# Full-row weights for one-row matmuls, crossbar transposes at two block boundaries, and another emission order, in a fused state-space and gated-MLP kernel

## Chip, cores and metric

One core of one Trainium2 chip. The metric is device time in microseconds (us) from start to end of one execution.

PE is TensorE's matmul side, PEld its weight load, DVE VectorE, ACT ScalarE, POOL GpSimd, SP the engine that issues DMAs here (SPq is its queue). L480 is line 480 of the kernel concerned. The kernels with padding have one line more above the matmuls, so L480 of the kernel before is L481 there.

## The reference

A pre-normalized state-space convolution with a residual, then a pre-normalized gated MLP with a residual, for 2048 positions of 640 channels:

```python
# u: (1, 2048, 640); A, B, C: (640, 128) complex
P = jnp.exp(logdA[:, :, None] * l[None, None, :])
K = jnp.einsum("dn,dnl,dn->dl", Cc, P, dB).real        # the taps
y = irfft2(rfft2(pad(u)) * rfft2(pad(K)))[..., :L] + u * Dskip
# ... cut ...
h  = x + ssm(layernorm(x))
h2 = h + (sigmoid(layernorm(h) @ w_gate) * (layernorm(h) @ w_up)) @ w_down   # F = 1728
```

## The kernel before

The kernel has two stages. Stage one builds tables and taps on DVE, ACT and PE, transforms the input (`forward`) and the taps (`spec`), and inverts block 0 of the result. Stage two runs the MLP on four blocks of 512 positions, in whose gaps PE inverts the next block from spectral products (`VR`) that DVE makes.

One-row matmuls: `one`, `last` and `sel` pick rows; `one` adds the skip term to tap 0, `last` adds edge taps, `sel` adds the edge term of block 0's last position.

```python
    sel[32, 0, 31] = 1.0
    # ... cut ...
    for c in range(4):
        last[c, 0, c, 0:4] = 1.0
        last[c, 1, c, 4:10] = 1.0
        last[c, 2, c, 10:14] = 1.0
    one[64, 0] = 1.0

        def diagonal(g1, kts):                       # 8 calls
            ps = ps2.tile([P, 2, 512], F32, name="ps_kv", tag="p2")
            # ... cut ...
            for c4 in range(4):
                for m in range(4):                   # L479: 128 rows, 32 columns
                    MM(pv[32 * m:32 * m + 32, :, :, c4], lhsT=pick[:, c4, :], rhs=kj[:, :, :, 4 * m + c4], start=not c4, stop=(m > 0 and c4 == 3), tile_position=(0, 32 * m))
            MM(pv[0:32, 0], lhsT=one[64:65, :], rhs=edge[64:65, dc]..., start=False, stop=True, tile_position=(64, 0))     # L480
            # ... cut: L482 ...
            nc.scalar.copy(kv[:, :, 4 * g1:4 * g1 + 4 * GC], ...)
            for q in range(2):                       # L485
                MM(ps[0:NL, 1, 0:4 * GC], lhsT=last[0:1, q, 0, :], rhs=kv[0:1, 3 + q, ...], start=False, stop=(q == 1))

    def inv0(c, ...):                                # 4 calls
        # ... cut ...
            if a:                                    # L550
                MM(ps[96:128, a, W:2 * W], lhsT=sel[32:33, 0, :], rhs=edge[32:33, o:o + W], start=False, stop=False, tile_position=(32, 96))
```

The order of stage one: every piece of work is a named unit with needs; of the units whose needs are met, the one with the lowest key in a table `AT` is emitted next. `s0` is the spectrum of the first 160 channels' taps for one lag, `l0` the same for the other lags, `p0` their product with the input's spectrum; `f1` and `f2` are the forward transforms of blocks 1 and 2.

```python
            unit(f"s{c}", f"k{c}d S01 f0 n0", L(corner, c), L(spec, c, 0, 0), L(spec, c, 0, 1))
            unit(f"p{c}", f"s{c}" + ..., L(prod, c, (0, 1)))
            unit(f"l{c}", f"s{c}", ...)              # spec of lags 1 to 3
    unit("ea1", "A1", L(exps_a, 1))                  # a burst of ACT exponentials
    units["ivh"] = (["f1", "f2"], (mk_iv,))
```

The boundary from one MLP block to the next. `DT` says for each block whether the crossbar transposes the normalized rows, `PW` which PSUM buffers are used:

```python
    def turn(b):
        lnT = lnTs[b] = xp.tile([P, 5, 4, 128], BF16, name="lnT", tag="G")
        if AT["DT"][b]:
            for i in range(4):
                nc.sync.dma_start(lnT[:, :, i, :], ln2[:, i, :], transpose=True)
            return
        if b and AT["PW"]:
            pts = [pso[0].tile([P, 4, 4, 128], BF16, name="ml_pt", tag="ml_po") for _ in range(2)]
            # ... 20 transposes on PE, three ACT copies ...
            return
        # ... otherwise five pieces of 4 transposes and a copy, in the gate's buffers ...

        for lp in (0, 2):                            # the down projection's halves
            if lp and AT["PW"]:                      # second half in the gate's and up's buffers
                po = [[p.tile(...) for _ in range(2)] for p, t in ((psg_p, "ml_pg"), (psu_p, "ml_pu"))]
            else:                                    # in the down projection's own two buffers
                po = [[t[:, c] for c in range(2)] for t in (pso_p.tile(...) for _ in range(2))]
            if not lp and b < NB - 1:
                prep(b + 1)                          # layer norm of the next block
            chunks(0, True, False)
            if lp and b < NB - 1:
                turn(b + 1)
            # ... 64-row tail, chunks(1, False, True) ...
            # ... for k, c:
                        tb = Wd[:, 15, 320 * c:320 * c + 320]
                        nc.scalar.copy(tb, po[k][c][:, 0:320])
```

## Time and profile before

| | before |
|---|---|
| time, median (range of four runs) | 361.31 us (360.59 to 361.48) |
| span of the profiled execution | 358.8 us |
| first large inverse of block 0 starts (L556) | 116.34 us |
| last inverse of block 0 has ended (first statistics of its result, L718) | 145.35 us |
| gate projection starts, blocks 1, 2, 3 (L898) | 206.26, 260.69, 310.71 us |
| last spectral products for block 3, start of the pair (L695) | 283.79 us |

These milestones are read from the timeline. They are a row of posts along the chain that ends last: a difference that appears between two posts was made there. Each is read from one execution. The busy shares and the chain are in the prediction. Columns of a timeline are start, duration, engine, line, operation, output and inputs, count, and in brackets the idle time ahead and what ended it.

### The profile page before, as it was taken

The numbers are of one execution on the slowest core, as the hardware profiler recorded it, in microseconds if no ns is written. First come the engines' busy times: TensorE is split into PE (matmuls) and PEld (weight loads), VectorE is DVE, ScalarE is ACT, GpSimd is POOL, SyncE is SP. The second block draws the span as 40 slices with busy tenths as digits, with TensorE's granted clock in tenths as the row PEclk, the third lists the DMA queues.
The fourth block names the chain that finished last, engine by engine and source line by source line (L and its number), as shares of the span: only waits on it lengthen the run. The fifth ranks groups of instructions, "written<-read, shape, count | busy, mean of one in ns | idle before, by whom it ended". The sixth has DMA issues, their size and how long they took to land.

```text
span 358.8 us, 6679 instructions
## 1 busy us (share of the span) xinstructions
PE 324.9 (91%) x2604; PEld 205.7 (57%) x2604; DVE 285.4 (80%) x597; ACT 245.0 (68%) x449; POOL 11.6 (3%) x19
## 2 busy tenths in 40 slices
PE   1598979899999999899999899998699999999995
PEld 1385646777586769744456544455444556644463
DVE  4899999999999979789998999998999931221221
ACT  6999997999899645662767755656655578655500
POOL 1011102000000000100001000001000001000000
PEclk9999999999999999999999999999899999999999
DMA  6990000257007159799400250000030000100011
GB/s 178 337 379 3 16 2 2 83 158 266 13 3 221 75 183 357 177 291 299 184 4 0 74 186 36 2 0 2 1 146 3 0 0 2 55 20 1 0 37 38
DMA packets 29703, 34.37 MB, mean 96 GB/s; under 512 B 16988, under 2 KB 25053, under 8 KB 29416
## 3 DMA queue, kind: packets, MB, share of 16 engines
q1 hardware_dynamic: 29672, 33.95, 29.1%
q8 instruction: 20, 0.33, 0.4%
q14 instruction: 11, 0.09, 0.1%
HBM read 24.72 MB, written 9.21 MB: 95 GB/s over the span
## 4 chain that ended last, share of the span: by engine, by line
PE 41%; DVE 32%; ACT 13%; DMA 7%; issue 3%; SPq 2%; POOL 1%; POOLq 0%; DVEq 0%; ACTq 0%
PE ml_pg L898 8%; PE ml_pu L898 8%; PE ml_po L931 6%; DVE u L684 4%; DVE u L685 4%; PE ps_z L449 3%; PE ps_y L556 3%; PE ps_xk L510 3%; DVE u L687 2%; DVE u L688 2%; PE ps_kv L479 2%; PE pk L468 2%; DVE ln_st L399 2%; ACT zs L450 2%; DMA raw<-in_A_C_re_dram 2%
## 5 line engine op out<-in xcount | busy, mean ns | idle before, releaser
L898 PE MATMUL ml_pg<-lnT,Wg 128*128 128x512 bf16 x260 | 64.8, 379 | 0.7 <-ACT ml_sg L906 0.7
L898 PE MATMUL ml_pu<-lnT,Wu 128*128 128x512 bf16 x260 | 64.9, 379 | 0.5 <-ACT Wd L952 0.4
L931 PE MATMUL ml_po<-Wd,ml_hm 128*128 128x320 bf16 x416 | 59.1, 301 | 0.0
L931 PEld LDWEIGHTS <-ml_hm 128*128 128x128 bf16 x416 | 40.1, 98 | 18.7 <-issue 2.4
L906 ACT ACTIVATE ml_sg<-ml_pg 128x512 bf16<-128x512 f32 x52 | 31.2, 599 | 26.0 <-PE ml_pg L898 14.6
L909 DVE TENSOR_TENSOR ml_hm<-ml_ub,ml_sg 128x512 bf16<-128x512 bf16 x52 | 21.8, 419 | 28.4 <-ACT ml_ub L908 28.4
L908 ACT CAST ml_ub<-ml_pu 128x512 bf16<-128x512 f32 x52 | 30.4, 585 | 20.4 <-PE ml_pu L898 20.2
L898 PEld LDWEIGHTS <-Wu 128*128 128x128 bf16 x260 | 25.4, 98 | 31.5 <-issue 1.0
L898 PEld LDWEIGHTS <-Wg 128*128 128x128 bf16 x260 | 25.4, 98 | 29.2 <-issue 0.9
L449 PE MATMUL ps_z<-u,c_G 128*128 128x320 bf16 x192 | 28.8, 298 | 2.2 <-ACT a_cs L273 0.7
L510 PE MATMUL ps_xk<-kv,c_KM 128*128 128x160 bf16 x320 | 26.6, 232 | 2.4 <-ACT zs L450 1.0
L684 DVE TENSOR_TENSOR u<-Z,S 128x1280 bf16<-128x1280 bf16 x34 | 27.7, 817 | 0.1
L685 DVE TENSOR_TENSOR u<-Z,S 128x1280 bf16<-128x1280 bf16 x34 | 27.7, 816 | 0.0
L246 PE MATMUL ps_t<-fr,c_dg 128*128 128x160 f16 (+1 forms) x180 | 20.0, 240 | 6.1 <-DMA c_dg<-s4c_dg 4.3
L510 PEld LDWEIGHTS <-c_KM 128*128 128x128 bf16 x320 | 23.1, 98 | 4.1 <-issue 3.2
L449 PEld LDWEIGHTS <-c_G 128*128 128x128 bf16 x192 | 18.4, 97 | 10.9 <-issue 3.9
L246 PEld LDWEIGHTS <-c_dg 128*128 128x128 f16 x180 | 14.8, 100 | 13.0 <-issue 4.9
L688 DVE TENSOR_TENSOR u<-u,u 128x1280 bf16<-128x1280 bf16 x23 | 18.8, 817 | 0.0
L687 DVE TENSOR_TENSOR u<-u,u 128x1280 bf16<-128x1280 bf16 x23 | 18.8, 816 | 0.0
L468 PE MATMUL pk<-tabB,tabA 128*128 128x84 bf16 x320 | 16.6, 200 | 2.3 <-ACT kts L469 2.0
L468 PEld LDWEIGHTS <-tabA 128*128 128x128 bf16 x320 | 14.4, 97 | 5.2 <-issue 4.3
L469 ACT CAST kts<-pk 128x420 bf16<-128x420 f32 x32 | 15.6, 543 | 2.5 <-PE pk L468 2.4
(157 smaller groups left out, 549.6 us busy)
## 6 DMA issues: line engine op xcount, KB each, us to landing
dz<-zs SPq DMA_DIRECT2D x12, 320.0 KB, 2.2
c_KM<-s4c_KM SPq DMA_DIRECT2D x1, 2560.0 KB, 12.8
dxk<-xk SPq DMA_DIRECT2D x16, 160.0 KB, 2.4
h<-in_A_u_dram SPq DMA_DIRECT2D x4, 640.0 KB, 3.9
eo<-dz SPq DMA_DIRECT2D x4, 640.0 KB, 4.6
S<-dxk SPq DMA_DIRECT2D x4, 640.0 KB, 7.4
Wg<-in_B_w_gate_dram SPq DMA_DIRECT2D x4, 520.0 KB, 7.9
Wu<-in_B_w_up_dram SPq DMA_DIRECT2D x4, 520.0 KB, 7.7
```

Source lines behind the costliest of these rows:

```text
L246: MM(ps[:, a, q * w:q * w + w], lhsT=dg[:, dk, :], rhs=fr[:, src, i, o + oo:o + oo + w], start=False, stop=(q == m - 1 and i == 1))
L449: MM(ps[:, ri, 0:UH], lhsT=G[:, ft, 0 if b in EO else hf, ri, r, :], rhs=us[b][:, r, o:o + UH], start=(r == rr[0]), stop=(r == rr[-1]))
L468: MM(pk[:, i, :], lhsT=A[:, ri, g].rearrange("p e c -> p (e c)"), rhs=B[:, ri, :, 4 * g:4 * g + 4], start=(ri == 0), stop=(ri == 1))
L510: mm = MM(ps[:, hf, ri * W:ri * W + W], lhsT=KM[:, ft, hf, ri, KI[d] + q, :], rhs=kv[:, j, :], start=(q == 0), stop=(q == len(KD[d]) - 1)).ins
L684: V(t1, z, k[:, :, :, hs_], ALU.mult)
L685: V(t2, z, k[:, :, ::-1, hs_], ALU.mult)
L687: V(s1, s1, t1, ALU.add)
L688: V(s2, s2, t2, ALU.add)
L898: nc.tensor.matmul(ps[:], lhsT=W[:, dc, f0:f0 + 128], rhs=lnT[:, dc].rearrange("p a b -> p (a b)"), start=(dc == 0), stop=(dc == 4))
L906: nc.scalar.activation(sg[:], pg[:], AF.Sigmoid)
L908: nc.scalar.copy(ub[:], pu[:])
L931: nc.tensor.matmul(po[k][c][:, 0:320], lhsT=hm[:, ft, 128 * lr:128 * lr + 128], rhs=Wd[:, ft, 320 * c:320 * c + 320], start=(start and ft ...
```

## The change

The intent: give the one-row matmuls all rows, with zero weights for those that do not matter, so that their weight loads need not idle ahead of them (0.37 us for L480 in the kernel before); take the transposes of blocks 2 and 3 off PE and ACT; and re-order stage one to suit. The diff, with `AT` cut (49 of its 59 keys change):

```diff
-AT = {... "bb2": 68.1, "ea1": 70.7, "ta2": 71.2, "s0": 66.5, "l0": -14.7, "p0": -14.4, "PW": 1,
-      "DT": (0, 0, 0, 0), "NA": (1, 2, 0, 0), "SA": (2, 0, 0, 3), "F": (-18.0, 64.3, 14.3, 46.5), ...}
+AT = {... "bb2": 68.7, "ea1": 70.7, "ta2": 72.8, "s0": 71.3, "l0": -17.5, "p0": 54.3, "PW": 0,
+      "DT": (0, 0, 1, 1), "NA": (1, 0, 1, 2), "SA": (1, 0, 0, 3), "F": (-59.9, 64.3, 14.3, 80.5), ...}
     for c in range(4):
-        last[c, 0, c, 0:4] = 1.0
-        last[c, 1, c, 4:10] = 1.0
         last[c, 2, c, 10:14] = 1.0
+    last[0, 0, 0, 0:4] = 1.0
+    last[0, 1, 0, 4:10] = 1.0
     edge = cp.tile([96, D], BF16, name="edge")
+    nc.gpsimd.memset(edge[:], 0.0)
-            MM(pv[0:32, 0], lhsT=one[64:65, :], rhs=edge[64:65, dc]..., tile_position=(64, 0))
+            MM(pv[0:32, 0], lhsT=one[0:96, :], rhs=edge[:, dc]..., tile_position=(0, 0))
-                MM(ps[0:NL, 1, 0:4 * GC], lhsT=last[0:1, q, 0, :], rhs=kv[0:1, 3 + q, ...], ...)
+                MM(ps[0:NL, 1, 0:4 * GC], lhsT=last[:, q, 0, :], rhs=kv[:, 3 + q, ...], ...)
-                MM(ps[96:128, a, W:2 * W], lhsT=sel[32:33, 0, :], rhs=edge[32:33, o:o + W], ..., tile_position=(32, 96))
+                MM(ps[96:128, a, W:2 * W], lhsT=sel[0:96, 0, :], rhs=edge[:, o:o + W], ..., tile_position=(0, 96))
-                        tb = Wd[:, 15, 320 * c:320 * c + 320]
+                        tb = Wd[:, 14 + k, 320 * c:320 * c + 320]
```

## The prediction

2.9 - 0.5 + 2.4 = 4.8 us, less 1.2 for the cap, plus 1.0 come to 4.6, so 361.4 - 4.6 = 356.8. "Drain" is what the trace shows at L480, an idle weight load of 0.37 us and 0.2 us of chain; that rows make it, and that all rows remove it, was inferred from the waits told beside it. The 0.15 for a pair of L485 was an estimate. The 0.07 of streaming is the pace of other 160-column matmuls of this trace (52 of L510 in 3.89 us). "For columns it shows" speaks of the trace, "This trace has none" of crossbar transposes.

> **What bounds the kernel now.** The kernel was timed at 361.38 us (median of three runs); its profiled execution spans 358.8 us. I read first the page's busy shares and its row of slices, then the table of 10-us stretches, then the chain of waits, and last the timeline of the places that the diff touches. Line numbers are those of the kernel before.
>
> ```profile
> PE 324.9 (91%) x2604; PEld 205.7 (57%) x2604; DVE 285.4 (80%) x597; ACT 245.0 (68%) x449; POOL 11.6 (3%) x19
> PE   1598979899999999899999899998699999999995
> DVE  4899999999999979789998999998999931221221
> ACT  6999997999899645662767755656655578655500
> ```
>
> There are two stages. In stage one (to about 149 us: tables, kernel taps, forward transforms, the inverse of block 0) PE, DVE and ACT are all nearly full. From the 10-us stretches, PE idles about 11 us between 20 and 150 us and DVE about 6.6 us. In stage two (four blocks of layer norm, gate and up projection, down projection) PE is full except at block boundaries, and DVE is full until about 285 us with the spectral products that later blocks need.
>
> The chain runs through DVE up to 51 us, through a mix of ACT and PE up to about 115 us, and from there to 145 us nearly only through PE. That is where the one-row matmuls stand (L480 and L485; L550 is the third kind):
>
> ```profile
> 118.73 0.86 PE ps_kv L479 x14
> 119.59 0.14 PE ps_kv L480
> 119.73 0.17 PE ps_kv L482 x2
> 119.98 0.76 PE ps_kv L479 x12
> 120.74 0.13 PE ps_kv L480
> 120.88 0.25 PE ps_kv L482 x4
> ```
>
> The timeline of the same place has the weight load of the one-row matmul idle for 0.37 us, not for data but for "issue", and the wait table repeats it for all three lines:
>
> ```profile
> 119.52 0.09 PEld L480 LDWEIGHTS <-c_one 1*32 1x32 bf16 x1 [0.37 <-issue]
> ```
>
> ```profile
> PEld L480 <- issue: 2.4, 7, 0.4
> ...
> PEld L485 <- issue: 1.4, 4, 0.4
> ...
> PEld L550 <- issue: 0.8, 3, 0.3
> ```
>
> In stage two the largest wait of PE is for the layer norm's transposes: "PE ml_pt L863 <- ACT Wd L952", 4.6 us in three waits: 1.8 us ahead of block 1, 2.7 ahead of block 2, 0.2 ahead of block 3. The boundary from block 1 to block 2:
>
> ```profile
> 253.50 0.72 ACT L952 CAST Wd<-ml_po 128x320 bf16<-128x320 f32 x2
> 254.28 1.87 PE L863 MATMUL ml_pt<-c_ident,ln 128*128 128x128 bf16 x16 [2.66 <-ACT Wd L952]
> 256.07 2.42 ACT L865 COPY lnT<-ml_pt 128x1024 bf16<-128x1024 bf16 x3 [1.85 <-PE ml_pt L863]
> 256.72 4.13 PE L931 MATMUL ml_po<-Wd,ml_hm 128*128 128x320 bf16 x26
> 260.69 1.24 PE L898 MATMUL ml_pg<-lnT,Wg 128*128 128x512 bf16 x5
> ```
>
> PE needs a buffer that ACT empties only after four normalizations (they end at 253.6), then transposes, then finishes the down projection, then starts block 2.
>
> [...] 0.26 to 0.37 us of idle load ahead of one-row and 64-row matmuls (L480, L485, L550, L942). For columns it shows next to nothing: L479 (128 rows, 32 columns) follows full-array matmuls without a recorded wait. So padding to all rows should remove the drain although the outputs stay 32 columns wide. [...] This trace has none; its nearest relative is an SBUF-side copy of the same 160 KB in rows of 320 bytes, which landed in 2.4 us:
>
> ```profile
> dxk<-xk SPq DMA_DIRECT2D x16, 160.0 KB, 2.4
> ```
>
> **The change part by part.** (1) Padding. 8 matmuls L480, 8 pairs L485 and 4 matmuls L550 get all rows (96 or 128), with zero weights. [...] The groups of four L479 start every 0.19 us (118.83, 119.02, 119.21), so L480 could have started at 119.40 and started at 119.53: 0.13 of drain. Its successor came 0.13 later where 0.05 is usual: 0.08. That is 0.2 us for one L480. I estimate 0.15 for a pair of L485 (0.16 in the chain [...]) and 0.2 for L550 (0.17 in the chain where 0.07 is streaming, plus what precedes it). Sum: 8 x 0.2 + 8 x 0.15 + 4 x 0.2 = 3.6 us of PE time. On the PE-only part of the chain after 115 us are 4 of each: 4 x 0.55 = 2.2 us. Of the other 1.4 I count half, as ACT often ends the wait there: 0.7. Together 2.9 us off stage one, if DVE follows. The cleared edge tile costs one GpSimd memset near the start, beside idle time.
>
> (2) Emission order. I compared what each engine does before fixed points, with this trace's durations. DVE's work before the first tap product (which opens the PE part) is 52.1 before and 51.8 after (nominal sums; operations overlap by about a tenth). One more statistics row and one normalization fewer on DVE add 0.8 nominal, about 0.7 us by the end of stage one. ACT loses about 1 us there, PE nothing. The number of ACT table loads stays four. So the order as such brings no work off any engine; I count it as +0.5 us, with an uncertainty of 2 to 3 us, because it may close or open some of DVE's 6 us of waits.
>
> (3) Transposes. Blocks 2 and 3 lose 20 transposes each on PE and three ACT copies (2.42 us), and get four crossbar DMAs each. The second half of each down projection now accumulates in the same two buffers as the first, in every block, not in the gate and up buffers. At the boundary to block 2: PE finishes its first half at 250.9 minus 3.6 = 247.3; the first buffer is emptied at 248.56, so PE waits 1.3 us, works 3.6 us to 252.2, and waits for the second buffer to 254.2 (the copies at 253.50). Then tail and last half, 0.4 + 3.6 us: free at 258.2 where before it was 260.7. Gain 2.4 us, if the transposes have landed by then. The last normalized row is there at 253.6, so they have 4.6 us; from the 2.4 us of the copy I expect 3 us for the last. At the boundary to block 3: transposes cost 1.4 us (305.25 to 306.80, less the down projection's own start), a new wait for the second buffer 0.3: gain 1.0 us, with 4.7 us of room. At the boundary to block 1 the transposes stay on PE, but in five pieces through two buffers, interleaved with five ACT copies; it loses about 0.5 us and saves the 0.4 us wait of the first up projection for its buffer: nothing. Block 3's end has no ACT copies and does not change. Sum: 3.4 us.
>
> **The cap.** PE can move forward only as far as DVE's products do.
>
> ```profile
> 283.79 0.88 DVE L695 TENSOR_TENSOR VR<-y 128x640 bf16<-128x640 bf16 x2
> ```
>
> They end at 284.67, and PE reads them in the third inverse group of block 2 at 286.60: 1.9 us of slack. Up to there the parts sum to 2.9 - 0.5 + 2.4 = 4.8 us. DVE must then come 2.9 us earlier, out of some 9 us of waits, with 0.7 us more work. I count 1.2 us of the 4.8 as lost to it: 3.6. With the 1.0 at the boundary to block 3: 4.6 us, so 361.4 - 4.6 = 356.8.
>
> **Rivals.** (a) Slow crossbar. [...] At three times the plain copy, 7 us for the last, each boundary gives back 2.4 us: about 361. [...] a tuned schedule that keeps such a loss is unlikely. (b) DVE is the bound. Its row is full from 20 to 285 us; then padding only turns PE work into PE waits for products, and the gain is the 1.9 us of slack and the 1.0 after it, less 0.7: about 359. (c) The drain is worth more than I read, or the new order packs DVE's waits well: all of the 3.6 us, and 4 of DVE's 9 us: about 351. (d) The column mode drains too once the row mode does not: part 1 is nothing, about 358.5.
>
> **Range and chances.** Rivals (b) and (d) lie within 2 us of the prediction; (c) is the lower end, a mildly slow crossbar the upper. Predicted 356.8 us, 8 in 10 between 351 and 363. Faster by over 2% means under 354.15, which needs 7.2 us: 0.21. Slower by over 2% means over 368.6, which needs the slow crossbar: 0.06. Within 2%: 0.73.
>
> **What would show it.** Right: no "issue" wait ahead of the loads of the padded matmuls, and about 0.2 us less at each on PE; PE's largest wait in stage two now for the down projection's buffer (1 to 3 us at the boundary to block 2); transposes landing within 4.6 us of the last normalization; a new or longer PE wait for VR in block 2. Wrong: gate matmuls of blocks 2 and 3 waiting for a DMA; the padded matmuls still idle for "issue"; stage one's end (the last block-0 inverse, 145.3 us now) earlier by over 5 us or later than now, which would make the emission order the main term.

## More of the kernel before

Every execution told here was at a mean granted TensorE clock of 0.99 to 1.00.

The kernel before:

```profile
62.05 1.79 PE L449 MATMUL ps_z<-u,c_G 128*128 128x320 bf16 x12 [0.17 <-ACT tabMB L273]
63.68 1.82 PE L510 MATMUL ps_xk<-kv,c_KM 128*128 128x160 bf16 x24
66.55 3.89 PE L510 MATMUL ps_xk<-kv,c_KM 128*128 128x160 bf16 x52 [1.04 <-ACT zs L450]
70.59 0.44 PE L510 MATMUL ps_xk<-kv,c_KM 128*128 128x160 bf16 x4 [0.16 <-ACT xk L514]
71.19 4.01 PE L449 MATMUL ps_z<-u,c_G 128*128 128x320 bf16 x28 [0.16 <-ACT xk L514]
```

Two kinds of work alternate: forward transforms (L449) and spectra of the taps (L510, units `s0` and `l0`, 80 matmuls here). The bracketed waits sum to 1.5 us.

## The result, and the profile after

The changed kernel ran in 358.73 us (median; 357.72, 358.83, 358.74, 358.71) against 361.31 before. The ratio is 0.9926, 95% interval 0.9904 to 0.9948. Ratios here are the mean time of one kernel's fast runs over that of the other's of the same rounds, so not quite the ratio of the medians. Correct, and inside 2%. The span of the profiled execution went from 358.8 to 355.9 us.

| milestone (start, us) | before | after | difference |
|---|---|---|---|
| first large inverse of block 0 | 116.34 | 118.31 | +1.97 |
| last inverse of block 0 has ended | 145.35 | 145.51 | +0.16 |
| gate of block 1 | 206.26 | 206.46 | +0.20 |
| gate of block 2 | 260.69 | 258.15 | -2.54 |
| gate of block 3 | 310.71 | 307.73 | -2.98 |

So stage one brought nothing, although PE should have had 2.9 us less to do there; the whole gain was made at the boundaries to blocks 2 and 3. The busy shares of the kernel after:

```profile
PE 322.0 (90%) x2564; PEld 203.5 (57%) x2564; DVE 286.2 (80%) x600; ACT 239.9 (67%) x442; POOL 11.0 (3%) x20
```

**The boundary to block 2.** The timeline of the kernel after:

```profile
251.16 5.29 SPq L858 DMA_TRANSPOSE lnT<-ln  x4
...
253.47 0.72 ACT L953 CAST Wd<-ml_po 128x320 bf16<-128x320 f32 x2
254.25 0.43 PE L943 MATMUL ml_po<-Wd,ml_hm 64*128 64x320 bf16 x3 [1.11 <-ACT Wd L953]
...
254.61 3.71 PE L932 MATMUL ml_po<-Wd,ml_hm 128*128 128x320 bf16 x26
258.15 1.03 PE L899 MATMUL ml_pg<-lnT,Wg 128*128 128x512 bf16 x4
```

PE's transposes are gone; what holds PE now is the copy that empties the down projection's buffer, for 1.11 us, as predicted. The SP queue spends 5.29 us on issuing four transposes of 128x640, 1.22 to 1.33 us each; the single plain DMAs on it from 200 to 310 us take 0.24 to 0.36 us each. The table of DMAs of the kernel after shows that each transpose landed about as fast as the plain copy of 160 KB (2.4 to 2.5 us):

```profile
lnT<-ln SPq DMA_TRANSPOSE x8, 2.6
```

Part of the gain here is the clock, which the prediction did not count. In a table of stretches the columns are the stretch, its length, the busy time of PE, PEld, DVE, ACT and POOL with instruction counts, then the granted clock, the DMA share and GB/s. The kernel before, just after PE's wait of 2.66 us:

```profile
254.00:256.00 2.00, 1.72 (x16) 1.60 (x15) 2.00 (x6) 0.23 (x1) 0.00 (x0) 0.55 0.00 0
```

The kernel after, in an earlier stretch behind PE waits of 0.31 and 1.22 us, and in the same one:

```profile
244.00:246.00 2.00, 2.00 (x9) 1.18 (x9) 2.00 (x6) 1.46 (x3) 0.00 (x0) 0.50 0.00 0
...
254.00:256.00 2.00, 1.75 (x14) 1.11 (x14) 2.00 (x5) 0.95 (x3) 0.00 (x0) 1.00 0.73 147
```

At the lower clock the kernel before took 1.87 us for 16 transposes (1.05 ahead of block 3), 0.71 for the tail (0.45 there) and 4.13 for the 26 matmuls that take 3.71 after: about 1.5 us. In the kernel after the low stretch costs nothing: from the gate of block 1 to that of block 2 it takes 51.69 us, and so does the kernel e, told below, whose clock is 1.00 from 242 to 248 us.

**The padding.** The chain of the kernel after, at the place whose chain before is in the prediction:

```profile
120.69 0.87 PE ps_kv L480 x12
121.56 0.02 PE ps_kv L481
121.58 0.08 PE ps_kv L483 x2
...
121.75 0.76 PE ps_kv L480 x13
122.50 0.04 PE ps_kv L481
122.54 0.16 PE ps_kv L483 x4
```

The one-row matmul's own step in the chain fell from 0.13 to 0.14 us to 0.02 to 0.04 us. From 118.73 to the end of the last step the chain took 2.40 us before; here, from 120.69 to 122.70, it took 2.01: 0.2 us less for each L480, the predicted size. The weight-load waits tell more. In the kernel after (columns: total us, times, longest) there is no such wait left for L481, where there were 2.4 us in seven, but the two other padded kinds are still there:

```profile
PEld L486 <- issue: 0.8, 2, 0.4
PEld L551 <- issue: 0.8, 3, 0.3
```

In the chain, a pair of L486 takes 0.17 us (122.85), as a pair of one-row L485 did (0.16), and L551 takes 0.17 as L550 did. L486 has fewer such waits than L485 (1.4 us in four), but in the kernel d, told below, it has 1.1 us in three. Only one of the three kinds got its gain.

**Stage one's middle.** PE of the kernel after in the 62 to 76 us shown above for the kernel before:

```profile
61.77 2.20 PE L450 MATMUL ps_z<-u,c_G 128*128 128x320 bf16 x15
65.59 4.01 PE L450 MATMUL ps_z<-u,c_G 128*128 128x320 bf16 x28 [1.62 <-ACT zs L451]
69.76 2.33 PE L450 MATMUL ps_z<-u,c_G 128*128 128x320 bf16 x16 [0.15 <-ACT zs L451]
72.82 2.20 PE L450 MATMUL ps_z<-u,c_G 128*128 128x320 bf16 x15 [0.73 <-ACT zs L451]
75.84 0.23 PE L469 MATMUL pk<-tabB,tabA 128*128 128x84 bf16 x2 [0.82 <-DVE tabB L392]
```

The spectra are gone from here: with key 71.3 instead of 66.5, unit `s0` and what hangs on it come after `ea1` (70.7) and after tap products (L469); they start at 82.42 us. PE has only forward transforms, each of which needs an ACT copy, and ACT opens `ea1` with a table load:

```profile
63.20 1.28 ACT L274 ACT_TABLE_LOAD   x1
```

The copies that end the wait of 1.62 us start at 64.87, behind this load and one exponential. The kernel before has the same load (1.28 us at 64.15), but 24 matmuls of spectra run meanwhile.

The bracketed waits sum to 3.3 us, 1.8 more than before. Over the longer stretch from 50 to 116 us, the table of stretches has for the kernel before

```profile
50.00:116.00 66.00, 61.23 (x746) 46.11 (x745) 64.23 (x135) 60.86 (x109) 2.48 (x2) 1.00 0.31 101
```

and for the kernel after

```profile
50.00:116.00 66.00, 58.87 (x722) 44.89 (x722) 63.53 (x134) 60.65 (x108) 2.90 (x3) 1.00 0.31 93
```

2.4 us less PE work done in the same time. That would cancel a padding gain of about 2 us. But it might also be rival (b): that padding only turned PE work into PE waits, since DVE is nearly full as well. Near 284.9 us PE does now wait for DVE's products, which had 1.9 us of slack before:

```profile
284.36 0.89 DVE L696 TENSOR_TENSOR VR<-y 128x640 bf16<-128x640 bf16 x2
...
284.89 0.98 PE L791 MATMUL ps_y<-VR,c_IV 128*128 128x320 bf16 x6 [0.40 <-DVE VR L696]
```

### The profile page after: what moved, and what is told of

Its sections match the earlier page's. It is cut to its first block, busy times and chain, and to the rows that moved or that the text cites. A ratio compares the mean times of both kernels' runs of the same rounds, so it can differ in the third digit from the quotient of the medians.

```text
span 355.9 us, 6598 instructions
## 1 busy us (share of the span) xinstructions
PE 322.0 (90%) x2564; PEld 203.5 (57%) x2564; DVE 286.2 (80%) x600; ACT 239.9 (67%) x442; POOL 11.0 (3%) x20
## 4 chain that ended last, share of the span: by engine, by line
DVE 41%; PE 30%; ACT 17%; DMA 6%; issue 3%; SPq 1%; POOL 1%; POOLq 0%; DVEq 0%; ACTq 0%
DVE u L686 7%; DVE u L685 6%; PE ml_pg L899 5%; PE ml_pu L899 5%; PE ml_po L932 5%; DVE u L689 4%; DVE u L688 4%; ACT zs L451 3%; DVE ml_hm L910 3%; DVE VR L696 3%; PE ps_xk L511 3%; PE pt L214 2%; DMA raw<-in_A_C_re_dram 2%; PE pk L469 2%; DMA dz<-zs 2%
## 5 line engine op out<-in xcount | busy, mean ns | idle before, releaser
L932 PE MATMUL ml_po<-Wd,ml_hm 128*128 128x320 bf16 x416 | 60.9, 304 | 0.8 <-ACT Wd L953 0.5
L469 PE MATMUL pk<-tabB,tabA 128*128 128x84 bf16 x320 | 16.9, 200 | 3.8 <-ACT kts L470 2.1
L469 PEld LDWEIGHTS <-tabA 128*128 128x128 bf16 x320 | 14.6, 97 | 7.3 <-issue 6.1
```

Of the source, the lines that this page charges most:

```text
L469: MM(pk[:, i, :], lhsT=A[:, ri, g].rearrange("p e c -> p (e c)"), rhs=B[:, ri, :, 4 * g:4 * g + 4], start=(ri == 0), stop=(ri == 1))
L932: nc.tensor.matmul(po[k][c][:, 0:320], lhsT=hm[:, ft, 128 * lr:128 * lr + 128], rhs=Wd[:, ft, 320 * c:320 * c + 320], start=(start and ft ...
```

## The experiments

Two theories. The order theory: padding gained what L480 shows, and the new emission order took it away again, by starving PE in stage one. The DVE theory: PE's gain cannot pass, because DVE's products set the pace; the order is innocent. Eleven kernels were run, all correct. The first eight shared a chip and its runs of the kernel before (359.1 to 362.4 us); the last three (h, i, k) ran on another chip, so they are compared with the others by their ratios.

| run | median us (range) | ratio to before, 95% interval | last inverse ended | gates of blocks 1, 2, 3 |
|---|---|---|---|---|
| a, padding only | 359.20 (358.89 to 360.78) | 0.9971 (0.9929 to 1.0014) | 143.62 | 204.54, 259.02, 309.05 |
| b, transposes only | 357.67 (357.16 to 357.85) | 0.9918 (0.9881 to 0.9955) | 145.83 | 206.87, 258.79, 307.82 |
| c, order only | 361.43 (360.77 to 363.27) | 1.0033 (0.9987 to 1.0078) | 147.10 | 207.93, 261.14, 311.76 |
| d, padding and transposes | 355.89 (355.76 to 355.99) | 0.9871 (0.9828 to 0.9914) | 143.86 | 204.88, 256.82, 305.85 |
| e, after, `s0` early | 356.06 (355.13 to 356.48) | 0.9867 (0.9822 to 0.9912) | 144.25 | 205.19, 256.88, 306.47 |
| f, d, `s0` late | 357.78 (357.35 to 359.20) | 0.9930 (0.9889 to 0.9971) | 145.39 | 206.41, 258.35, 307.36 |
| g, d, wide edge term | 355.85 (355.13 to 356.69) | 0.9870 (0.9831 to 0.9910) | 144.78 | 205.81, 257.74, 306.76 |
| j, d, crossbar for block 1 too | 359.33 (359.13 to 362.46) | 0.9987 (0.9932 to 1.0041) | 143.77 | 203.67, 259.40, 309.39 |
| h, d, old buffers | 356.74 (354.97 to 357.20) | 0.9878 (0.9850 to 0.9905) | 144.02 | 204.9, 256.62, 307.02 |
| i, before, buffers only | 359.91 (359.62 to 360.17) | 0.9978 (0.9954 to 1.0002) | 145.42 | 206.4, 259.5, 309.7 |
| k, d, edge term of one row | 356.34 (355.81 to 357.26) | 0.9880 (0.9857 to 0.9904) | 144.6 | 205.7, 257.6, 306.6 |

Two cautions. The posts drift between executions: b and i have the stage one of the kernel before, and h and j that of d, yet the first large inverse starts at 116.34, 116.83, 116.41 and at 115.56, 116.20, 115.79. So differences of half a microsecond say nothing. And the times of the kernel before fall into two groups: in these rounds its five runs at a mean clock of 1.00 took 359.06 to 359.77 us, its fourteen at 0.989 to 0.995 took 360.24 to 362.42. A gain against it is thus partly a matter of which runs it met.

### a, b, c: each part alone

a, the kernel before with the padding:

```diff
+    last[0, 0, 0, 0:4] = 1.0   # ... and the other padding lines of the change; AT as before
```

> Only the one-row matmuls are padded; order, transposes and buffers as before. Theory 1 (the parts add up): the PE-only stretch from the first big block of L556 to the last inverse of block 0 (28.9 us before, 27.1 in the changed kernel) shortens by about 1.8 us, the end with it: 359.4 us. Rival (padding turns PE work into waits): stretch shorter, end unchanged, 361.3. Rival 2 (the drain is not the row count): stretch unchanged at 28.9.

b, the kernel before with the transposes and the buffers:

```diff
-      "PW": 1, "DT": (0, 0, 0, 0)
+      "PW": 0, "DT": (0, 0, 1, 1)
-                        tb = Wd[:, 15, ...]
+                        tb = Wd[:, 14 + k, ...]
```

> Only the crossbar transposes of blocks 2 and 3 and the down projection's buffers; stage one as before. Theory 1: 3.2 us at the two boundaries, 358.1 us; the crossbar lands 2.6 us after issue, 1.27 us between issues, as in the changed kernel. Theory 2 (the products of DVE cap it): 1.9 us up to 286 us and 1.1 after, 358.3, with a PE wait for VR in block 2.

c, the kernel before with the new `AT`, but the old `PW` and `DT`:

```diff
-AT = {...}   # of before
+AT = {...}   # of after, with "PW": 1, "DT": (0, 0, 0, 0)
```

> Only the new emission order and the moved statistics rows. Theory 1: the order costs the 2.0 us by which the changed kernel is late at its first big block of L556 (118.4 for 116.4 us): 363.3 us. Rival (the order is neutral, the delay came from the padding's added waits): 361.3.

Padding alone ended stage one 1.73 us earlier than before. In time it was 1.0 us (0.29% of 360.55, the median of before in these rounds), with an interval that includes zero. The stretch from the first large inverse on shortened by 1.2 us (29.0 to 27.8), not by the 1.8 expected. Transposes alone gained 3.0 us (0.82%), and b's milestones put the gain at the two boundaries, with no PE wait for VR. The order alone started the first large inverse 2.7 us later (119.01) and ended stage one 1.75 us later; the 1.2 us in time (0.33%) are not significant by themselves. So stage one of the changed kernel is the sum of a and c, -1.73 + 1.75, and nothing is left for DVE to explain.

### d: the change without its order

```diff
-AT = {...}   # of after
+AT = {...}   # of before, with "PW": 0, "DT": (0, 0, 1, 1)
```

> Padding and transposes with the old order. Theory 1: 361.3 - 1.8 - 3.2 = 356.3 us. Theory 2 (DVE caps): DVE's products still end near 284.7 us, PE waits for VR 2 us or more in block 2, 358.3 us.

355.89 us, all four runs within 0.23 us: 1.3% below before (ratio 0.9871, where the changed kernel has 0.9926). The DVE theory falls. PE did not wait for VR at all, and DVE came 1.5 us earlier than in the kernel before (282.29 against 283.79): it followed PE's gain instead of stopping it. Since a and b sum to 4.0 us and d gained 4.7, no loss to a cap shows.

### e and f: one key

e takes the changed kernel and puts only `s0` back; f takes d and moves only `s0` late.

```diff
-      "s0": 71.3          # e, in the kernel after
+      "s0": 66.5
```

> The changed kernel with one number of the order set back: the taps' spectrum of chunk 0 and its far lags (units s0, l0, p0) come right after the forward transforms of block 1 again, not after those of block 2. Theory: their late place is what made stage one 2 us longer, so 358.7 - 2 = 356.7 us, first big block of L557 near 116.3 instead of 118.3. Rival (the loss lies in other moves of the order): 358.7.

```diff
-      "s0": 66.5          # f, in the kernel d
+      "s0": 71.15
```

> The opposite: padding and transposes with the old order (355.9 us), only s0, l0 and p0 moved to where the changed kernel has them. Theory: about 2 us slower, 357.9. Rival: unchanged, 355.9.

One number brought the changed kernel from a ratio of 0.9926 to 0.9867, 2.1 us, and took d from 355.89 to 357.78 us, 1.9 us. In time that is, both ways and within the intervals, the whole difference between the two orders. At the posts it is most of it: at the end of stage one the changed kernel is 1.65 us behind d; `s0` early gains 1.26 of that (e), `s0` late costs 1.53 (f). But the first large inverse of e, expected near 116.3, starts at 117.36, only 0.95 earlier than in the changed kernel and 1.80 behind d; e makes up 1.4 of this by the end of stage one. So the other 46 changed order keys delay that post and give the time back after it; which of them do, was not tried. e's timeline in stage one has the spectra back among the transforms:

```profile
66.14 0.70 PE L450 MATMUL ps_z<-u,c_G 128*128 128x320 bf16 x4 [1.62 <-ACT zs L451]
66.73 5.14 PE L511 MATMUL ps_xk<-kv,c_KM 128*128 128x160 bf16 x72
```

The wait of 1.62 us stays in e, so the wait behind the table load is not what `s0` changes. What it changes shows some 10 us later, at the tap products. f has by then run all the forward transforms at hand, and waits for ACT's copies of the tap products:

```profile
77.40 0.95 PE L469 MATMUL pk<-tabB,tabA 128*128 128x84 bf16 x20 [1.11 <-ACT kts L470]
78.83 0.95 PE L469 MATMUL pk<-tabB,tabA 128*128 128x84 bf16 x20 [0.47 <-ACT kts L470]
```

d has transforms left to run there:

```profile
77.11 6.27 PE L450 MATMUL ps_z<-u,c_G 128*128 128x320 bf16 x44
```

From 76 to 90 us PE is busy for 13.78 us in d and 12.26 in f. Shown is the cause, the place of `s0`; that these waits are the whole of its cost was not taken apart.

### g and k: the padded matmul that still waits

L551 (96 rows, 32 columns, among matmuls of 128 columns) still idles for issue (0.8 us in three, in d). g pads its columns as well, with a 32-row constant that has a single one at column 127:

```diff
-                MM(ps[96:128, a, W:2 * W], lhsT=sel[0:96, 0, :], rhs=edge[:, o:o + W], ..., tile_position=(0, 96))
+                MM(ps[:, a, W:2 * W], lhsT=selw[0:96, :], rhs=edge[:, o:o + W], ...)   # selw: 128 columns
```

> Padding and transposes with the old order, and the edge matmul of the inverse (L551) padded in its columns too, 128 instead of 32 at a column position. The padded L551 still sat idle for 'issue' three times, 0.8 us in all. Theory (a change of column tile inside a stream of full-array matmuls costs the same wait): the wait goes, 0.4 to 0.8 us less, 355.3. Rival (the wait is something else): wait and time as in the kernel without it, 355.9.

The issue wait is gone from g's list of weight-load waits, and PE is faster there: from the two matmuls ahead of it to the large inverse it takes 0.34 and 0.36 us the first two times (115.35 to 115.69, 128.91 to 129.27), where d takes 0.53 and 0.56. The time did not fall: 355.85 against 355.89. Ahead of the last inverse g has, in the table of PE's waits,

```profile
PE ps_y L560 <- DVE V L533: 1.7, 1, 1.7
```

where d waits 0.42 us. DVE's product came at 141.66 instead of 140.74, as DVE had waited 1.36 us for a load (`eo`) where d waits 0.40. So in this execution a late load took what PE had gained; whether the widening pays without it is not shown. k puts L551 back to one row:

```diff
-                MM(ps[96:128, a, W:2 * W], lhsT=sel[0:96, 0, :], rhs=edge[:, o:o + W], ..., tile_position=(0, 96))
+                MM(ps[96:128, a, W:2 * W], lhsT=sel[32:33, 0, :], rhs=edge[32:33, o:o + W], ..., tile_position=(32, 96))
```

> The kernel with padding, crossbar and the old order (355.89 us), with one of the three padded kinds put back: the edge term of the last block's inverse (four matmuls of 32 columns at column position 96) has one row again. Theory 1 (its padding buys nothing, since its load still idles 0.26 us for issue in the padded kernel, three times): same, 355.6 to 356.2 us, and the PEld issue wait of that line stays 0.8 us in three. Theory 2 (the padding was worth the 0.2 us each that the prediction counted): 356.5 to 356.9 us and an issue wait of about 0.35 us or more each.

k's weight-load wait for this line is the same with one row as with 96:

```profile
PEld L551 <- issue: 0.8, 3, 0.3
```

Its ratio (0.9880) is d's (0.9871) within the intervals. Its median, 356.34, lies between the two expectations, but these were set by d's time on the other chip. The place itself decides: from the matmuls ahead of it to the large inverse PE takes 0.53 and 0.54 us in k (115.94 to 116.47, 129.71 to 130.25), as in d. From the first large inverse to the end of the last it took no longer than d (28.2 against 28.3 us). Padding the rows of L551 bought nothing.

### h, i, j: what the boundary hangs on

h is d with the second half of the down projection in the gate's and up's buffers again, so that PE need not wait for the copies:

```diff
-      "PW": 0
+      "PW": 1
```

> The kernel with padding, crossbar and the old order (355.89 us), but with the second half of each down projection back in the buffers of the gate and up projections. Theory 1 (at the boundary to block 2 the copies that empty the down projection's buffer end at 254.2, and PE, which waits 1 us for them, sets the start of block 2): with other buffers that wait goes, PE is free about 1 us earlier at the boundary to block 2, but the transposes, unchanged, land about 0.4 us before the old start, so the gain is limited to about 0.4 us there and about 0.3 at the boundary to block 3: 355.2 to 355.9 us, and the gate matmuls now wait for a DMA. Theory 2 (the pooled buffers of gate and up are freed late, so the second half waits for those instead, or the next block's gate finds no free buffer): 356.5 to 358.5 us, with a new PE wait for such a buffer.

h's timeline of PE at the boundary to block 2:

```profile
249.85 3.71 PE L932 MATMUL ml_po<-Wd,ml_hm 128*128 128x320 bf16 x26
256.62 1.24 PE L899 MATMUL ml_pg<-lnT,Wg 128*128 128x512 bf16 x4 [3.06 <-DMA lnT<-ln]
257.70 2.29 PE L899 MATMUL ml_pu<-lnT,Wu 128*128 128x512 bf16 x5
259.78 1.93 PE L899 MATMUL ml_pg<-lnT,Wg 128*128 128x512 bf16 x5
261.55 1.24 PE L899 MATMUL ml_pu<-lnT,Wu 128*128 128x512 bf16 x5
```

PE was done 3 us early, and then the transposes were what it waited for: they landed at 256.6, so in d, whose block 2 starts at 256.82, they have only 0.2 us to spare. That part of the first theory held. What neither theory had: after the 3.06 us of idleness the next groups of five ran at about half speed, 2.08 and 1.77 us from start to start where 1.08 is usual, 1.7 us lost. The table of stretches of h has the granted clock at 0.62:

```profile
257.00:260.00 3.00, 2.95 (x10) 1.13 (x9) 3.00 (x6) 0.60 (x1) 0.00 (x0) 0.62 0.09 36
```

In d, whose wait at this place is 1.09 us, the same stretch has 1.00. d has a low stretch too, earlier: a mean of 0.83 from 240 to 250 us, in which PE waits 2.0 us. There it cost nothing: f has a wait of the same length at the same line (L943) and 1.00 from 210 to 262 us, and both take 51.94 us from the gate of block 1 to that of block 2. So the length of the last wait does not decide alone. The clock fell after PE waits of 3.06 us (h), 2.66 (kernel before, 0.55 from 254 to 256 us), 2.0 (d) and 1.22 with 0.31 just before (kernel after, 0.50 from 244 to 246); it did not after 2.0 us in f, nor after 1.79 us ahead of block 1 in the kernel before (1.00 from 200 to 206). What decides it, these runs do not show. In time h (ratio 0.9878) and d (0.9871) do not differ beyond the intervals.

i is the kernel before with the down projection's own buffers for both halves, and no crossbar:

```diff
-      "PW": 1                      # before
+      "PW": 0
-                        tb = Wd[:, 15, ...]
+                        tb = Wd[:, 14 + k, ...]
```

> The kernel before with one thing changed: the second half of each down projection accumulates in the two buffers of the first; no crossbar, no padding, the old order. Theory 1 (the gain at the boundaries comes from taking the transposes and their copies out of PE's and ACT's way): the transposes still stand at the boundaries, PE waits for the down projection's buffer as well as for the copies of the transposes, so no gain: 361 to 363 us against 361.3 before, gate of block 2 at 260.7 or later. Theory 2 (the gain comes from the buffers, as PE no longer waits for gate and up buffers): most of the 3 us are here too: 358 to 359 us.

Neither theory. Block 2 starts 1.2 us earlier than before (259.49), block 3 1.0 us earlier; in time 0.8 us, an interval that just includes zero. i's timeline shows why: with this flag the transposes stay on PE but come in small pieces, between the down projection's matmuls.

```profile
253.84 0.45 PE L870 MATMUL ml_pt<-c_ident,ln 128*128 128x128 bf16 x5 [0.58 <-ACT ln L848]
254.23 0.55 PE L942 MATMUL ml_po<-Wd,ml_hm 64*128 64x320 bf16 x3
254.95 0.38 PE L870 MATMUL ml_pt<-c_ident,ln 128*128 128x128 bf16 x4 [0.17 <-ACT lnT L872]
255.26 0.31 PE L942 MATMUL ml_po<-Wd,ml_hm 64*128 64x320 bf16 x1
```

There is no long wait, and the clock is 1.00 from 252 to 260 us (24 matmuls of L931 in 3.42 us), where the kernel before had its low stretch. Counted by the posts from the gate of block 1 to that of block 3, i gains 1.2 us and b 3.5: about a third comes with the flag, all of it at block 2, and two thirds with the crossbar. In time this split is not resolved.

j gives block 1 the crossbar as well:

```diff
-      "DT": (0, 0, 1, 1)
+      "DT": (0, 1, 1, 1)
```

> Padding and transposes with the old order, and block 1 by the crossbar too. If the boundary to block 1 behaves like that to block 2, its gate matmuls start about 2 us earlier and the end moves with them: 354 us. Rival: the queue of DMA issues, now held by the transposes (5.2 us), delays the load of Z for block 3, DVE falls behind and PE waits for VR: 356 or more.

Block 1 itself starts 1.2 us earlier (203.67 against d's 204.88), and then the kernel is 3.4 us slower. j's timeline:

```profile
196.68 5.29 SPq L858 DMA_TRANSPOSE lnT<-ln  x4
203.47 7.07 SPq L663 DMA_DIRECT2D eo<-dz  x2
...
208.40 0.83 DVE L665 TENSOR_TENSOR Z<-eo 128x1280 bf16<-128x1280 bf16 x1 [3.15 <-DMA eo<-dz]
```

The loads of block 3's input spectrum (`eo`) now stand behind the transposes in SP's queue, and the chain has the first of them start only when the last transpose has landed:

```profile
200.74 2.59 DMA lnT<-ln
...
203.47 4.91 DMA eo<-dz
```

In d the first is issued at 201.85. DVE waits 3.8 us in all for them, which it does not in d, and its last products start at 286.02 instead of 282.29. From there everything is late: PE waits 1.5 us for VR, and blocks 2 and 3 start 2.6 and 3.5 us later than in d. The rival of the expectation came true. DVE's cap exists; it binds when DVE itself is held up.

## Why the prediction was right or wrong

The prediction said 356.8 and the chip 358.7: within the range, and in the band that it gave 0.73. The gain was 2.7 us (0.74%) where the sum had 4.6.

| term of the sum | predicted | measured |
|---|---|---|
| (1) padding, off stage one | -2.9 | -1.0 (a, in time), -1.8 (b to d), -1.7 (a, at the end of stage one) |
| (2) emission order | +0.5 | `s0` alone: +2.1 (after to e), +1.9 (d to f); all of it: +2.0 (after to d, by ratios), +1.65 (the same, at the end of stage one), +1.2 (c, in time, not significant) |
| (3) transposes and buffers | -3.4 | -3.0 (b, in time), -3.3 (a to d) |
| the cap by DVE | +1.2 | 0 (d) |

**The failed step is (2), the emission order.** The prediction compared how much work each engine has before fixed points, found that "the order as such brings no work off any engine", and gave it +0.5 us with an uncertainty of 2 to 3. The true size lay inside that uncertainty, but the reasoning could not find it: the loss is in which work PE still has to run when it would otherwise wait for ACT (f: 1.11 and 0.47 us between tap products, where d runs 44 transforms), not in sums. Most of it came from one move, unit `s0` behind `ea1`, which the diff of `AT` shows. The prediction's own sign for it came true, too: it named as wrong a stage one that ended "later than now", which "would make the emission order the main term", and it ended 0.16 us later. That is inside the drift of the posts; the sign that counts is that stage one gained nothing.

**Step (1) was right for one kind of three.** The 0.2 us for each L480 is what the chain shows, and 8 x 0.2 = 1.6 us is about all that padding gave. The 0.15 for a pair of L485 and the 0.2 for L550 were not there, and both padded kinds still idled for "issue", which the prediction had named as a sign of being wrong. (The sum counts a matmul's own time as the same with all rows, which was an estimate; it held: L551 takes 0.24 us with 96 rows in d and with one in k.) "So padding to all rows should remove the drain although the outputs stay 32 columns wide" held where the neighbours are 32 columns wide as well (L480 among L479: of 2.4 us of issue wait none is left). L551 stands among 128-column matmuls, and its wait, 0.8 us in three with 96 rows (d) and with one (k), went only when its columns were widened too (g); rival (d) was right for this kind. L486 (14 columns, after matmuls of 128 columns) fits the same reading but was not tried. That the first 32-column matmul after a full one shows no wait in the trace, as the prediction noted, stays unexplained. Where this wait went, in g, the 0.2 us were there on PE (0.53 to 0.34), but the time did not fall.

**Step (3) was right.** Measured from the gate of block 1 on, so that stage one does not count, the boundary to block 2 was predicted to gain 2.4 us and gained 2.74 in the kernel after and 2.51 in b; the boundary to block 3 was predicted to gain 1.0 and gained 0.44 and 0.99 (the difference of the gates' starts, before less after). Part of this was luck: 1.2 to 1.5 us of the old boundary to block 2 were the low clock, which the prediction took for work. c has the old boundary at a clock of 1.00 from 254 to 262 us (16 transposes in 1.05 us, 26 matmuls in 3.71) and takes 53.21 us from gate to gate, where the kernel before takes 54.43 and the kernel after, in the same order as c, 51.69: the transposes by themselves are worth about 1.5 us there. The two waits for the down projection's buffers were to be 1.3 and 2.0 us (252.2 to 254.2). In the kernel after the first is missing and the second is 1.11: PE ran the matmuls ahead of them at a clock of 0.50 to 0.65 (244 to 248 us) and came late to both. In e and f, at a clock of 1.00 there, they are 0.87 and 1.74 (1.73 in f). One term was too small and did no harm: the last transpose was to land 3 us after the last normalization. In h that row ended at 252.26 and the last transpose landed at 256.6, 4.4 us, since four issues of about 1.27 us follow each other on SP before the 2.6 us of the last. The room was put at 4.6. Rival (a), the slow crossbar, is refuted by the 2.6 us.

**The cap** was argued from a slack of 1.9 us, and would have had DVE gain less than PE. DVE's products came earlier by the same 1.5 us as stage one (d), since what they wait for comes earlier. PE did wait 0.40 us for them in the changed kernel, where the new order had delayed DVE again (its last products start at 284.36, in a at 282.13). That rival (b) is out is shown by d.

Two errors made the prediction too fast: padding too large by some 1.1 to 1.9 us and the order's cost too small by about 1.5. The cap of 1.2 us, which did not bind, took back part of them, and that the result lies within 2 us of the prediction is luck to that extent.

## What to carry to other kernels

When a change bundles a re-ordering with real savings, compare engine by engine which work is left to fill the places where another engine is waited for, not only how much work there is; then run the change without its order. Here padding rows paid where the neighbours had the same column tile (L480, 0.2 us each) and not where they were wider (L550, 0.8 us of issue wait with one row and with 96): look at the neighbours before counting on it. Look at the granted clock behind each long wait before putting a boundary's cost down to its instructions: here 1.2 to 1.5 us of one boundary were a clock of 0.55 to 0.59. The transposes that left PE for a DMA queue took issue time there, 5.29 us for four, and delayed later loads enough to cost 3.4 us in j: ask what stands behind a transpose in that queue, and put it only where nothing urgent does.
